# Forgetting attention and a two-layer GELU network on one core: rebuilt fronts of the first two batches, another order in a second GEMM, and earlier loads

## The chip, the cores and the metric

The kernel runs on one core of a Trainium2 chip. The metric is the device time of one execution in microseconds (us); less is better. The kernel before was timed three times: 337.19, 337.76 and 339.93 us, median 337.76. The engines are named as in the profile: PE (TensorE, matmul), PEld (its weight load), DVE (VectorE), ACT (ScalarE), POOL (GpSimd) and SP (SyncE, which here only issues DMAs).

## The reference

```python
# q, k, v: [8, 8, 576, 64], f: [8, 8, 576] in 0.8..1.0
scores = scale * q @ k.T
cum    = cumsum(log(clip(f, 1e-4, 1)))
scores = where(causal, -1e9, scores + cum[:, None] - cum[None, :])
attn   = softmax(scores)                 # per batch and head
x      = (attn @ v) -> [8 * 576, 512]
out    = gelu(x @ w_in) @ w_out          # w_in [512, 2048], w_out [2048, 512]
```

The term of the query in the decay cancels in the softmax. So the kernel multiplies v by a weight for each key, which is proportional to exp(-cum), carries the weight itself as a 65th column of v, and divides by that column's sum at the end.

## The kernel before

**Tiling.** Work goes batch by batch. The eight heads of a batch are four pairs (i = 0 to 3). The 576 keys are five blocks of 128 (the last two overlap by 64 keys). For each pair, `scores` makes four tiles of scores (t = 0 to 3) on PE into the two-buffer PSUM pool "s"; ACT takes the exponential of each tile; the causal mask is laid on afterwards by POOL (`affine_select`, L312), or beforehand by small extra matmuls on PE where `on_pe` holds. `attend` multiplies the exponentials with the weighted v (`vw`), one head at a time, into pool "o"; `normalize` (two DVE instructions) gives x. x is transposed into xT, by PE and a copy in batches 0 and 1, by a DMA on SP in the others. Then the first GEMM (`gemm1`, 16 steps of four matmuls, each with a GELU on ACT) makes the tiles g. The second GEMM (`gemm2_...`) of a batch runs as filler between the score tiles of the next batch: `take(fill, n)` issues its next n steps.

The last 64 rows of each batch are gathered in `tails` and go through both GEMMs at the end of the kernel.

**PSUM.** There are three pools of two buffers: "s", "o" and "m". A new tile in a pool waits until the tile two places before it has been read.

**The order of work.** Every engine works its own instructions in the order in which the code issues them, which is written out by hand. The queues matter as much as the engines:

- SP issues the loads of v (`load_v`, L120, five DMAs for each call, one for each block of keys), the transposes by DMA (`transpose_dma` L236, `x_dma` L370) and the stores of the output (`store`, L506).
- POOL issues the loads of q and k (`load_qk_tokens`, L108), of w_in in four quarters (L172) and of w_out in four quarters (L176). Between these it weighs v (`weigh_v`, L269 and L276) and masks (L312). A tiny copy holds its queue until a transfer has landed (`gate` L568, `behind` L573).
- There is one v_sb. A new batch of v can be loaded only after `weigh_v` has read the old one.

**The front, batch 0 (`first_attention`).** ACT takes the log of f (L187), DVE sums it up (L189), ACT takes the exponential (L588, L191 brings its table), PE transposes the weights (L598). q and k of each pair are transposed by PE (`transposes_first`) and copied by DVE, or by ACT for the first pair (L217 to L222). After `gate`, POOL issues the loads of w_in, v and q, k of batch 1, and the first quarter of w_out.

**Batch 1 (`second_attention`).** Filler is `gemm2_first(0)`: for the row blocks ts = 0 and 1 of batch 0, the steps kt = 0 to 7 of sixteen. This uses the first two quarters of w_out (kt 0 to 3 and 4 to 7). The last two quarters are loaded near its end.

**Batch 2.** Filler is `gemm2_third`: `gemm2_second(0)` (kt 8 to 15 for ts 0 and 1), then PLAN_0 (all of kt for ts 2 and 3 of batch 0), then PLAN_1 (batch 1). A step marked "r" in a plan is two matmuls of 64 rows each into two banks; one marked "n" is one of 128 rows. The two banks are copied and added by DVE into a tile `ot` (pool "outs", four buffers) and stored. Batch 2 gives 48 filler steps before its first `attend`. In the first GEMM of batch 1 the code also issues `weigh_v` for the pairs 0 and 1 of batch 2, then the loads of q and k of batch 3.

Of the kernel before, what the change touches and what calls it, by code (L numbers as in the profile page):

```python
# [12 lines left out]
Alu = mybir.AluOpType  # L13
# [40 lines left out]
def kernel(  # L54
# [100 lines left out]
    e4 = [consts.tile([P, 2, 448], BF16, name=f"e4{i}") for i in range(4)]  # L155
    for t in e4:
        nc.gpsimd.memset(t[:, :, 0:D], 0.0)
    diagonal(ident_fp, Alu.not_equal, 1.0, 0)
    load_qk_tokens(0, 6, 8)
# [20 lines left out]
    ones = consts.tile([BH, S], FP32)  # L180
    lf = f_sb
    cum = consts.tile([BH, S], FP32)
    wk = f_sb
    nc.vector.memset(ones, 1.0)
    nc.vector.memset(wT[0:D, 4, :], 0.0)
    nc.vector.tensor_scalar(f_sb, f_sb, 1e-4, 1.0, Alu.max, Alu.min)
    nc.scalar.activation(lf, f_sb, Act.Ln)  # L187
    nc.vector.memset(v_sb[0:D, :, 4, :], 0.0)
    nc.vector.tensor_tensor_scan(cum, ones, lf, 0.0, Alu.mult, Alu.add)  # L189
    spark = consts.tile([1, 1], FP32)  # L190
    nc.scalar.activation(spark, ones[0:1, 0:1], Act.Exp)  # L191

    def warm_up(n):

        ps = m_psum.tile([P, TC], FP32, tag="m", name="ps_w")
        for _ in range(n):
            nc.tensor.matmul(ps, warm[:, 0:P], warm, start=True, stop=True)
# [4 lines left out]
    def transposes_first(b, i, which, pool, tag):  # L202
# [12 lines left out]
        src = ps.rearrange("d j p -> d p j")  # L215
        if b or i:
# [9 lines left out]
    def transpose_dma(b, h0, h1):  # L226
# [8 lines left out]
        for src, dst in zip(qk_of[b], tq_of[b]):  # L235
            nc.sync.dma_start_transpose(  # L236
                dst[:, h0:h1].rearrange("d h j p -> d (h j) p"),
                src[:, h0:h1].rearrange("p h c -> p (h c)"),
            )
# [24 lines left out]
    def weigh_v(b, i, eng=nc.gpsimd):  # L264
# [3 lines left out]
        w = wT[:, :, bh : bh + 2].rearrange("p n h -> p h n")  # L268
        eng.tensor_tensor(  # L269
            vw(b)[:, hs, :, 0:D],  # L270
            v_sb[:, hs, :, :],
            w.unsqueeze(3).to_broadcast([P, 2, NBLK, D]),
# [7 lines left out]
    def scores(b, i, t):  # L280
        on_pe = b == 0 or (b == 1 and i == 0)
# [42 lines left out]
    def attend(b, i, h, ms):  # L324
        if (b, i, h) not in o_of:
            o_of[b, i, h] = o_psum.tile([P, NBLK, D + 1], FP32, tag="o", name="o")
# [125 lines left out]
    PLAN_0 = [(2, "o", 16 * "r"), (3, "m", 14 * "r" + 2 * "n")]  # L452
# [55 lines left out]
    ot_of = []  # L508

    def gemm2_first(c):  # L510

        pss = [
            m_psum.tile([P, d_model], FP32, tag="m", name="ps2") for _ in range(2)
        ]
        for kq in (0, 4):
            for ts in range(2):
                for kt in range(kq, kq + 4):
                    nc.tensor.matmul(  # L518
                        pss[ts],
# [3 lines left out]
                        stop=(kt == 7),  # L523
                    )
                    if kt == 7:
                        ot_of.append(
                            o_pool.tile([P, d_model], FP32, tag="ot", name="ot")
                        )
                        copy = nc.scalar.copy if ts else nc.vector.tensor_copy
                        copy(ot_of[ts], pss[ts])  # L530
                    yield

    def gemm2_second(c):

        for ts, pool, tag in ((0, o_psum, "o"), (1, m_psum, "m")):
            banks = [
                pool.tile([P, d_model], FP32, tag=tag, name="ps2") for _ in range(2)
            ]
            for kt in range(8, n_ff):
                for r in range(2):  # L540
                    rows = slice(r * D, (r + 1) * D)
                    nc.tensor.matmul(  # L542
                        banks[r],
                        g_of[c][kt][rows, ts * P : (ts + 1) * P],
                        w_out_sb[rows, kt, :],
# [300 lines left out]
```

## Time and profile before

| | us |
|---|---|
| Runs | 337.19, 337.76, 339.93 |
| The profiled execution's own time | 337.49 |
| Span of its profile (first to last instruction) | 335.5 |
| PE busy in the span | 326.8 |
| ACT busy | 209.2 |
| DVE busy | 181.2 |
| POOL busy | 122.4 |

The granted clock of TensorE was 0.997 over the span. The profile is read in this order: the page gives the share of each engine; the chain of waits tells in which stretch something other than PE sets the pace; the timeline of one engine gives single instructions, with the idle time ahead of them and what ended it; the DMA view of a narrow window gives one transfer's time from issue to landing. All times are from the start of the span.

### The profile page before, as it was taken

What the parts mean: (1) busy time and instruction counts of PE and PEld (TensorE: products, weight loads), DVE (VectorE), ACT (ScalarE), POOL (GpSimd) and SP (SyncE); (2) the same over time, 40 slices, a digit from 0 to 9 for tenths busy, and PEclk for the clock granted to TensorE, in tenths of its full rate; (3) what the DMA queues carried; (4) which work ended last, traced back from release to release, by engine and by line L of the source; (5) the groups of instructions that cost most, each with busy time, mean ns of one, the idle gap of its engine ahead of it and who ended that gap; (6) DMA issues with size and microseconds to landing.
All of it is one profiled execution on the core that took longest, in us unless ns stands there. A gap on an engine that the chain in (4) does not pass through costs nothing.

```text
span 335.5 us, 7820 instructions
## 1 busy us (share of the span) xinstructions
PE 326.8 (97%) x3161; PEld 171.2 (51%) x3161; DVE 181.2 (54%) x414; ACT 209.2 (62%) x299; POOL 122.4 (36%) x250
## 2 busy tenths in 40 slices
PE   8799989999999999999999999999999999999995
PEld 3574546445554456445644565446544654444443
DVE  4770456684358945894589547964696550020011
ACT  6977797773734787378827891788378846404600
POOL 8190286038437044723463343624351420000000
PEclk9999999999999999999999999999999999999998
DMA  7999999989999799599949698689800241011013
GB/s 113 188 166 191 206 172 165 193 157 169 206 197 177 119 198 189 102 141 148 224 120 141 136 179 174 87 158 211 140 35 2 83 64 61 0 66 62 0 41 84
DMA packets 104627, 44.16 MB, mean 132 GB/s; under 512 B 83408, under 2 KB 100048, under 8 KB 104592
## 3 DMA queue, kind: packets, MB, share of 16 engines
q1 hardware_dynamic: 87296, 29.52, 46.4%
q0 software_dynamic: 16896, 13.63, 27.6%
q8 instruction: 24, 0.39, 0.5%
q10 hardware_dynamic: 400, 0.52, 0.4%
q14 instruction: 11, 0.09, 0.1%
HBM read 36.85 MB, written 9.44 MB: 138 GB/s over the span
## 4 chain that ended last, share of the span: by engine, by line
PE 83%; DMA 10%; POOL 3%; issue 1%; ACT 1%; DVE 1%; SPq 0%; POOLq 0%; DVEq 0%; ACTq 0%
PE ps L386 33%; PE ps L482 26%; PE ps L422 8%; PE o L331 7%; PE s L300 6%; DMA w_out_sb<-in_moe_w_out_dram 6%; DMA xT<-x 2%; DMA v_sb<-in_v_dram 2%; PE ps L542 1%; PE ps L518 1%; POOL q L108 1%; POOL k L108 1%; ACT e L310 1%; POOL vw L269 0%; SPq L120 0%
## 5 line engine op out<-in xcount | busy, mean ns | idle before, releaser
L406 ACT ACTIVATE g<-ps 128x512 bf16<-128x512 f32 x144 | 82.1, 601 | 83.7 <-PE ps L386 83.7
L310 ACT ACTIVATE e<-s 128x896 bf16<-128x896 f32 (+2 forms) x128 | 100.1, 835 | 20.9 <-PE s L300 18.2
L386 PE MATMUL ps<-xT,w_in_sb 128*128 128x512 bf16 x512 | 112.7, 379 | 0.1
L482 PE MATMUL ps<-w_out_sb,g 64*128 64x512 bf16 (+1 forms) x711 | 108.1, 377 | 0.0
L386 PEld LDWEIGHTS <-w_in_sb 128*128 128x128 bf16 x576 | 55.9, 98 | 67.8 <-issue 2.1
L312 POOL TENSOR_SCALAR_AFFINE_SELECT e<-e 128x256 bf16<-128x256 bf16 (+1 forms) x135 | 49.3, 386 | 86.9 <-ACT e L310 86.6
L482 PEld LDWEIGHTS <-g 64*128 64x128 bf16 (+1 forms) x711 | 39.4, 95 | 34.7 <-issue 4.2
L269 POOL TENSOR_TENSOR vw<-v_sb,wT 128x640 bf16<-128x640 f32 x30 | 38.7, 1290 | 26.0 <-DMA v_sb<-in_v_dram 14.7
L300 PE MATMUL s<-qT,kT 64*128 64x320 bf16 (+4 forms) x384 | 43.8, 276 | 2.2 <-ACT e L310 1.3
L250 DVE COPY kT<-tk 64x288 bf16<-64x288 bf16 x96 | 43.9, 458 | 2.3 <-DMA tk<-k 0.7
L250 DVE COPY qT<-tq 64x288 bf16<-64x288 bf16 x96 | 38.8, 404 | 3.7 <-DMA tq<-q 2.3
L490 DVE COPY ot<-ps 128x512 f32<-128x512 f32 x20 | 13.8, 692 | 47.2 <-PE ps L482 47.2
L331 PEld LDWEIGHTS <-e 128*128 128x128 bf16 x960 | 34.5, 98 | 8.6 <-POOL e L312 2.5
L331 PE MATMUL o<-vw,e 128*128 128x65 bf16 x960 | 37.4, 194 | 0.5 <-DVE vw L269 0.5
L345 DVE TENSOR_TENSOR x<-o,r 128x320 bf16<-128x320 f32 x64 | 31.5, 492 | 3.3 <-DMA xT<-x 1.1
L431 DVE COPY ot<-ps 128x512 f32<-128x512 f32 (+2 forms) x9 | 5.7, 633 | 49.6 <-PE ps L422 49.6
L300 PEld LDWEIGHTS <-kT 64*128 64x128 bf16 x384 | 19.6, 94 | 24.1 <-issue 7.6
L422 PE MATMUL ps<-w_out_sb,g 128*128 128x512 bf16 (+2 forms) x144 | 28.0, 355 | 0.0
L422 PEld LDWEIGHTS <-g 128*128 128x128 bf16 x144 | 13.5, 98 | 14.5
L344 DVE RECIPROCAL r<-o 128x5 f32<-128x5 f32 x64 | 12.1, 189 | 12.2 <-PE o L331 12.1
L502 DVE TENSOR_TENSOR ot<-ot,ps 128x512 f32<-128x512 f32 x22 | 15.1, 685 | 1.1
L386 PE MATMUL ps<-tails,w_in_sb 128*128 128x512 bf16 x64 | 14.3, 378 | 0.0
(69 smaller groups left out, 137.5 us busy)
## 6 DMA issues: line engine op xcount, KB each, us to landing
out_dram<-ot SPq DMA_DIRECT2D x32, 256.0 KB, 2.5
v_sb<-in_v_dram SPq DMA_DIRECT2D x24, 256.0 KB, 4.6
q<-in_q_dram POOLq DMA_DIRECT2D x6, 576.0 KB, 6.3
k<-in_k_dram POOLq DMA_DIRECT2D x6, 576.0 KB, 8.2
v_sb<-in_v_dram SPq DMA_DIRECT2D x22, 128.0 KB, 4.6
w_in_sb<-in_moe_w_in_dram POOLq DMA_DIRECT2D x4, 512.0 KB, 8.2
w_out_sb<-in_moe_w_out_dram POOLq DMA_DIRECT2D x4, 512.0 KB, 8.6
q<-in_q_dram POOLq DMA_DIRECT2D x4, 144.0 KB, 4.5
```

The lines of the kernel that those rows point to most:

```text
L250: nc.vector.tensor_copy(rows[:, odd], src[odd * D : (odd + 1) * D, 2 * i + h].rearrange("d j p -> d p j"),)
L269: eng.tensor_tensor(vw(b)[:, hs, :, 0:D], v_sb[:, hs, :, :], w.unsqueeze(3).to_broadcast([P, 2, NBLK, D]), Alu.mult,)
L300: nc.tensor.matmul(to, *ab, start=half < 0, stop=half == 1 or not masked)
L310: nc.scalar.activation(et[:, :, z:c], st[:, :, z:c], Act.Exp, scale=scale)
L312: nc.gpsimd.affine_select(out=et[:, :, c0 + z : c0 + P], in_=et[:, :, c0 + z : c0 + P], compare_op=Alu.is_ge, fill=0.0, base=z, pattern=[[ ...
L331: nc.tensor.matmul(o[:, m, :], e_of[b, i, t][:, h, c : c + P], vw_of[b][:, 2 * i + h, n, :], start=(n == 0), stop=(n == m),)
L345: nc.vector.tensor_tensor(x_of[b, i][:, :, h, :], o[:, :, 0:D], r.unsqueeze(2).to_broadcast([P, NBLK, D]), Alu.mult,)
L386: nc.tensor.matmul(ps, w_in_sb[:, kt, ffb * P : (ffb + 1) * P], src[:, kt, 0:TC], start=(kt == 0), stop=(kt == n_dm - 1),)
L406: nc.scalar.activation(g_of[c][ffb], ps, Act.Gelu)
L422: nc.tensor.matmul(pss[ts][:, c0:c1], g_of[c][kt][:, ts * P : (ts + 1) * P], w_out_sb[:, kt, c0:c1], start=(kt == 0), stop=(kt == n_ff - 1),)
L482: nc.tensor.matmul(banks[r], g_of[c][kt][rows, ts * P : (ts + 1) * P], w_out_sb[rows, kt, :], start=kt == (steps.index("r") if r else 0), ...
L502: nc.vector.tensor_tensor(ot, ot, bank, Alu.add)
```

## The change

It does the following.

- **Weights of v (batch 0).** The log, the running sum and the exponential are replaced by one running product on DVE, from the last key backwards, that starts at 2^80. ACT loads one table instead of two at the start. The filling of four tiles `e4` and of others with zeros moves from POOL to DVE; the loads of the last q and k of batch 0 move ahead of it on POOL.
- **Order in batch 0.** The transposes of q and k are put one at a time between score tiles; the copy of the last k comes behind the weighing of pair 0, which is done in two parts (four blocks, then the last one); the two heads of a pair are attended one after the other, pair 1 in pool "m".
- **Loads for batch 1.** v of batch 1 is loaded as two heads, then two, then four, instead of four and four. The second quarter of w_out moves from the end of batch 0's GEMM to the end of batch 1's attention, where the other two quarters stand. q of batch 2 keeps its place; k of batch 2 is issued later by POOL, behind the masks of pair 1.
- **Order in batch 1.** The third set of transposes comes behind the tiles of pair 0; the masks of pair 3 are made by PE; both heads of pair 3 are attended before the third transpose of x. The table of GELU is brought by an extra tiny activation.
- **Second GEMM of batch 0.** In batch 1 the filler takes kt 0 to 3 for all four ts (also sixteen steps). In batch 2 `gemm2_second` takes the other 48: kt 4 to 7 for ts 0 and 1, kt 8 to 15 for these, then kt 4 to 15 for ts 2, then for ts 3.
- **v of batch 2, and q, k, v of batch 3.** `load_v(2)` moves from the end of batch 1's attention to a place behind the transposes by DMA of q and k of batch 2, which now go q, q, k, k. All four `weigh_v` of batch 2 stand in the first GEMM of batch 1, the loads of q and k of batch 3 between the second and the third. `load_v(3)` stands at the end of that GEMM instead of behind the first `attend` of batch 2.

```diff
-    for t in e4:
-        nc.gpsimd.memset(t[:, :, 0:D], 0.0)
+    load_qk_tokens(0, 6, 8)
     diagonal(ident_fp, Alu.not_equal, 1.0, 0)
-    load_qk_tokens(0, 6, 8)
...
-    nc.scalar.activation(lf, f_sb, Act.Ln)
-    nc.vector.tensor_tensor_scan(cum, ones, lf, 0.0, Alu.mult, Alu.add)
...
-    def scores(b, i, t):
-        on_pe = b == 0 or (b == 1 and i == 0)
+        on_pe = b == 0 or (b == 1 and i in (0, HP - 1))
...
     def gemm2_third():
         yield from gemm2_second(0)
-        yield from gemm2_rows(0, PLAN_0)
         yield from gemm2_rows(1, PLAN_1)
...
-        nc.scalar.activation(
-            wk, cum, Act.Exp, bias=cum[:, S // 2 : S // 2 + 1], scale=-1.0
-        )
-        warm_up(2)
+        nc.vector.tensor_tensor_scan(
+            decay[:, S - 2 :: -1], f_sb[:, S - 1 : 0 : -1], none[:, 0 : S - 1],
+            2.0**80, Alu.mult, Alu.add,
+        )
+        warm_up(2, 2 * P)
...
-        transposes_first(0, 3, 1, m_psum, "m")
-        weigh_v(0, 0, nc.vector)
+        copy = transposes_first(0, 3, 1, m_psum, "m", late=True)
+        weigh_v(0, 0, nc.vector, 0, NBLK - 1)
+        weigh_v(0, 0, nc.vector, NBLK - 1)
+        copy()
...
-        load_v(1, 0, 4)
+        load_v(1, 0, 2)
...
-        heads = [(i, h) for i in range(3) for h in range(2)]
-        for i, t in ((2, 2), (2, 3), (3, 0), (3, 1), (3, 2), (3, 3)):
-            scores(0, i, t)
-            attend_head(*heads.pop(0))
+        scores(0, 2, 2)
+        for ms in ((0, 1, 2, 3), (4,)):
+            for h in range(2):
+                attend(0, 0, h, ms)
+        for h in range(2):
+            normalize(0, 0, h)
+        scores(0, 2, 3)
+        scores(0, 3, 0)
+        for h in range(2):
+            attend_head(1, h, m_psum, "m")
+        scores(0, 3, 1)
+        scores(0, 3, 2)
+        for h in range(2):
+            attend_head(2, h)
+        scores(0, 3, 3)
...
         tiles(0, 0)
-        transposes(1, o_psum, "o")
-        transposes(2, m_psum, "m")
+        transposes(1, m_psum, "m")
+        transposes(2, o_psum, "o")
+        tiles(0, 2)
         transposes(3, o_psum, "o")
-        tiles(0, 2)
         take(fill, 2)
...
         take(fill, 4)
+        load_qk_tokens(2, which="k")
         weigh_v(1, 2)
...
         tiles(3, 0)
-        transpose_dma(2, 0, 4)
-        transpose_dma(2, 4, 8)
+        for n in range(2):
+            transpose_dma(2, 0, 4, (n,))
+            transpose_dma(2, 4, 8, (n,))
+        load_v(2)
...
         tiles(3, 2)
+        nc.scalar.activation(warm[0:1, 0:1], warm[0:1, 0:1], Act.Gelu)
         behind(qk_of[2][1], H - 1)
+        load_w_out(1)
         load_w_out(2)
         load_w_out(3)
         run(2)
         take(fill, 4)
-        av(3, 0)
+        run(3)
...
-        av(3, 1)
...
-        load_v(2)
...
                 if ffb == 12:
                     behind(qk_of[1][0], H - 1)
+                    load_v(1, 2, 4)
                     load_v(1, 4, 8)
                     weigh_v(1, 0)
-                    load_w_out(1)
                     weigh_v(1, 1)
-                    load_qk_tokens(2)
+                    load_qk_tokens(2, which="q")
...
-                if late == gap - 2 and (b > 1 or at < 2):
+                if late == gap - 2:
                     weigh_v(b + 1, at)
                 if ffb == (9 if b == 1 else 14):
                     load_qk_tokens(b + 2)
+                if b == 1 and ffb == n_ff - 1:
+                    load_v(3)
```

In `attention(2)` the calls `load_v(3)` behind the first `attend`, and `weigh_v(2, 2)` and `weigh_v(2, 3)` behind the tiles of pair 0, are gone. The new heart of `gemm2_second`, in short:

```python
order = [(ts, kt) for two in ((0, 1), (2, 3)) for kq in (0, 8) for ts in two
         for kt in range(kq, kq + 8) if kt >= 4]
order.sort(key=lambda at: (2, 3).index(at[0]) if at[0] in (2, 3) else -1)
# ts 0 and 2 in pool "o", ts 1 and 3 in pool "m"; DVE adds both banks to ot, SP stores it
```

## The prediction

> **What bounds the kernel now.** First the page: engine shares.
>
> ```profile
> PE 326.8 (97%) x3161; PEld 171.2 (51%) x3161; DVE 181.2 (54%) x414; ACT 209.2 (62%) x299; POOL 122.4 (36%) x250
> ```
>
> PE is idle for 335.5 - 326.8 = 8.7 us in all. Second, the busy times by stage (width, then PE, PEld, DVE, ACT, POOL, granted clock, DMA share, GB/s), to see where.
>
> ```profile
> 5.20:16.00 10.80, 8.82 (x188) 6.24 (x188) 7.33 (x13) 10.55 (x16) 4.01 (x13) 1.00 1.09 192
> 39.00:57.00 18.00, 16.62 (x289) 10.40 (x282) 10.78 (x25) 15.70 (x21) 15.02 (x29) 1.00 1.17 176
> 70.20:101.70 31.50, 31.50 (x367) 16.55 (x366) 15.71 (x35) 16.45 (x19) 15.84 (x32) 1.00 0.97 177
> ```
>
> The front of batch 0 has 1.98 us to give and batch 1 some 1.4. Batch 2 has nothing: each wait put there lengthens the run. Third, the timeline of the front: the last two waits of PE and the steps on ACT that go.
>
> ```profile
> 4.04 0.68 ACT L187 ACTIVATE f_sb<-f_sb 64x576 f32<-64x576 f32 x1 [1.95 <-DVE f_sb L186]
> 4.74 1.28 ACT L191 ACT_TABLE_LOAD   x1
> 6.91 0.40 ACT L220 COPY kT<-ps_f 128x288 bf16<-128x288 bf16 x1
> 7.20 0.77 ACT L588 ACTIVATE f_sb<-cum 64x576 f32<-64x576 f32 x1
> 7.88 8.63 ACT L310 ACTIVATE e<-s 128x896 bf16<-128x896 f32 x11
> ...
> 15.05 0.37 PE L300 MATMUL s<-qT,kT 64*128 64x448 bf16 x2 [0.33 <-ACT e L310]
> 16.01 0.63 PE L331 MATMUL o<-vw,e 128*128 128x65 bf16 x15 [0.51 <-DVE vw L269]
> ```
>
> Fourth, batch 2: POOL's and SP's queues and the DVE copy that frees PE's banks.
>
> ```profile
> 72.87 1.28 POOL L269 TENSOR_TENSOR vw<-v_sb,wT 128x640 bf16<-128x640 f32 x1 [14.67 <-DMA v_sb<-in_v_dram]
> 75.62 0.84 POOL L108 DMA_DIRECT2D q<-in_q_dram  x1
> 77.23 1.73 POOL L312 TENSOR_SCALAR_AFFINE_SELECT e<-e 128x256 bf16<-128x256 bf16 x5
> 78.94 1.27 POOL L269 TENSOR_TENSOR vw<-v_sb,wT 128x640 bf16<-128x640 f32 x1
> ```
> ```profile
> 73.67 9.45 SPq L506 DMA_DIRECT2D out_dram<-ot  x4
> 84.18 2.18 SPq L370 DMA_TRANSPOSE xT<-x  x1
> 86.45 4.51 SPq L120 DMA_DIRECT2D v_sb<-in_v_dram  x5
> ```
> ```profile
> 86.58 0.69 DVE L490 COPY ot<-ps 128x512 f32<-128x512 f32 x1 [2.56 <-PE ps L482]
> 87.38 0.69 DVE L502 TENSOR_TENSOR ot<-ot,ps 128x512 f32<-128x512 f32 x1
> ```
>
> POOL waits 14.67 us for v of batch 2. The four stores of batch 0 are out of SP's queue before v of batch 3 enters it. The copy at 86.58 is the first that uses an `ot` tile a second time (four buffers), so it needs the first store landed; the sum behind it ends at 88.07, and PE takes the same two banks again at 88.16. No slack there. Fifth, the DMA queues while both carry data, 32 to 36 us (q0 POOL's, q1 SP's), and SP's alone, 66.2 to 72.
>
> ```profile
> q0 software_dynamic: 776, 0.57, 91.3%
> q1 hardware_dynamic: 772, 0.19, 36.5%
> ```
> ```profile
> q1 hardware_dynamic: 5140, 1.29, 130.6%
> ```
>
> Beside POOL's queue SP's moves 0.19 MB in 4 us (48 GB/s), alone 1.29 in 5.8 (222).
>
> **The change part by part.** The sum is made against the profiled execution's 337.49 (span 335.5 and 1.99 around it); the median of the runs, 337.76, is 0.27 above.
>
> *Front of batch 0.* The log (0.68), a table (1.28) and an exponential (0.77) leave ACT. Most of it was cover time: the first tile needs the second half of kT, which ACT copies at 6.91 when DVE's half is done, unchanged. Its scores are done at 7.70, so the first exponential starts at some 7.72 instead of 7.88: 0.16. The running product is one DVE scan, as before (1.35), now behind the kT copy: 6.9 to 8.25, when DVE has no other work until 8.31. The zero fills on DVE (eight of 0.1 to 0.5) lie in its wait for f until 3.56. Weighing pair 0 no longer stands behind the last kT copy (14.46 to 15.22): DVE's four blocks 14.1 to 14.8, the last when it lands (14.75) by 15.0; PE then goes on after its tile at 15.27 instead of 16.01: 0.74. From there PE's work is the same 8.2 us to 24.24, but the last tile's exponential now ends some 0.1 later than the third pair leaves PE. Gain 0.64; bounds 0 (last block of v 0.7 later, since q and k of pair 3 enter POOL's queue 0.95 earlier) and 1.95 (all gaps).
>
> *Batch 1.* v for heads 2 to 7 is moved behind q, so w_out's first quarter lands earlier (42.66 before) and PE's 0.44 us wait for it goes; what is late next is the third set of transposes, which now stands ahead of that place and waits for the copies of the second, with the same end. The extra masks (four small matmuls for a diagonal) put 0.12 behind PE's last tile; attending both heads first gives 0.12 back (wait of the last transpose for x). The GELU table (1.28) was hidden under PE's first matmuls already. On POOL the issue of k (0.78) comes between masks and weighing: last mask of pair 2 at 52.4 where 52.05 was, PE would want it at 52.2. So +0.2; bounds -1.2 (ACT's four gaps) and +1.0 (first rival below). Copies of `ot` on DVE: two more of 0.69, DVE has 7.2 us free here.
>
> *w_out.* Three quarters instead of two issue at some 53.4; two landed 6.8 and 10.3 us after their issue, 4.25 apart. The third lands by 69, needed at 72.5 (twelve steps of 0.216 into batch 2). Nothing. The filler of batch 2 is 48 steps both times: nothing.
>
> *v of batch 2 and SP's queue: the term that decides.* v(2) enters SP's queue earlier, but the bytes ahead of it are the same: the second quarter of w_out is moved into its path. The DMAs are at 90% or more all the way from 30 to 72 us but for some 1.9 us at 54 to 57, and the new order makes a hole of its own, while POOL waits for v's heads 2 and 3 before it issues q(2). It landed at 72.71. I take 72.3 (the exponentials ahead of k's issue are 0.6 earlier); ends 70.8 (no hole) and 75 (three quarters at 4.25 after 53.4, then the 7.1 us that v took after w_out before). POOL then weighs two pairs, issues q and k, weighs two more (before: 72.87 to 77.23, and 2.65 for two): v_sb is free at 79.5, and only then does SP issue `load_v(3)`. In the changed program its five loads stand ahead of the four stores of batch 0, which want to leave at 73.67. From first issue to last landing these five took 7.75 us undisturbed (86.45 to 94.20) and 10.1 in batch 3 (119.35 to 129.46), where a store issued right behind landed 0.27 after them. Here k of batch 3 shares the DMAs (it landed at 85.71) for some 3 us, at 48 instead of 222 GB/s: 7.75 + 3 x 0.78 = 10.05. The first store lands at 79.55 + 10.05 + 0.27 = 89.9, and the copy due at 86.58 starts then: +3.3 on PE. Queued behind it on DVE: the sum, then the normalizing of pair 1; who waits is PE, for both banks, and everything after it. As the copy now hangs on DMAs, the 0.4 gained ahead is lost in the same wait. Ends: no stall (v at 70.8 and 7.75: 86.1), and +5.7 (v at 75).
>
> [...] In this trace the store behind v in batch 3 landed after it. [...]
>
> Sum: 337.49 + 3.3 = 340.8.
>
> **The rivals.** (1) *The stores are in time*: v(2) lands below 69, or overtaking. Decides when the first store lands before 86. For it: v enters SP's queue earlier. Against it: the same bytes, DMAs full. Then the front's gain stays: 337.49 - 0.64 + 0.2 = 337.05, down to 335.5 if batch 1 gains too. This is the other side. (2) *POOL late in batch 1*: v of heads 2 and 3 is issued only after q's landing (38.34 before); if it lands later than 42.5, weighing (1.5), q(2) and the five masks (1.7) push the attend of pair 1, 1 us for each. For it: such loads took 4.5 us then. Against: the POOL queue is then empty. 338.0 if the stores are in time. (3) *Masks of batch 2 late*: all four weighings now stand ahead; masks end 9.1 us after v(2) lands, PE wants them at 81.2; above 72.1 it is the wait that shows first. Alone: 337.5 at 72.7. (4) *Wide DMA delay*: v(2) at 75 or w_out late: 343.2.
>
> **How the numbers follow.** Forecast (stores late by 1 to 5 us) 0.70; rival 1 0.19; rivals 2 and 3 without it 0.06; rival 4 0.05. Within 1% is about what a measurement can tell from no change: against 337.76 this is 334.4 to 341.1, so the forecast stands near its edge. Of its 0.70, 0.35 is above 341.1 (v(2) landing above 72.6); with 0.05 of rival 4 and 0.01, slower is 0.41. Faster by over 1% needs batch 1 to give over 2 us: 0.03. Within 1%: 0.56. The range goes from 336.5 (rival 1 with half of what batch 1 can give) to 343.0 (v(2) near 75); the forecast's own is 338.5 to 343.
>
> **What would show it.** Right: the DVE copy of `ot` in the first row block of PLAN_1 idle until a DMA of `out_dram`, PE idle some 3 us behind it near 88 us, SP's five loads of v ahead of four stores near 80; PE's first attend near 15.3; no wait of PE for w_out at 42.7. Wrong: v(2) landed and weighed before 70, the four stores out by 76, batch 2 without idle time on PE; or the loss in batch 1 at the attend of pair 1 or 2.

## The result and the profile after

The changed kernel takes 347.65 us (median of 6 runs, 346.40 to 348.56), the kernel before 338.06 (6 runs): ratio 1.028 with a 95% interval of 1.024 to 1.031. The forecast was 340.8 with a range to 343.0. The sign and the place were right, the size was not. Here and below a ratio is to the kernel before, run beside it on the same chip; it is taken by rounds and leaves disturbed executions out (e5's profiled execution is one of these), so that it can differ from the ratio of the medians.

The profiled execution of the changed kernel took 348.56 us, that of the kernel before 337.49: 11.07 more. First the engine shares on the page of the changed kernel, and the row of its clock in 40 slices of 8.7 us.

```profile
PE 326.9 (94%) x3139; PEld 173.5 (50%) x3179; DVE 181.9 (52%) x422; ACT 206.7 (60%) x297; POOL 119.8 (35%) x241
...
PEclk9999999999889999999999999999999999999999
```

PE's busy time on the page is that of before (326.8), but that can't be read as "all of the loss is idle time": the page has 3139 matmuls beside 3179 weight loads, so records are missing, and part of the busy time now runs at half clock (slices 11 and 12, 87 to 104 us). The busy times by stage (same columns as before) say where the loss lies.

```profile
5.20:16.00 10.80, 9.17 (x214) 6.67 (x214) 7.75 (x13) 9.36 (x13) 3.28 (x8) 1.00 1.04 180
39.00:57.00 18.00, 15.84 (x307) 10.97 (x311) 12.03 (x28) 16.45 (x23) 12.05 (x24) 1.00 0.98 153
70.82:102.00 31.18, 25.37 (x249) 12.96 (x252) 14.85 (x36) 12.39 (x15) 12.48 (x25) 0.89 0.88 169
```

Batch 2, where PE had no idle time before, now has 5.8 us of it, at a mean clock of 0.89. By the first score matmuls of each batch in the timeline, batch 2 begins at 70.82 (before 70.10) and lasts 55.61 us (45.37). So 0.72 comes ahead of it, 10.24 in it, 0.39 behind it, and -0.28 outside the span: 11.07.

The chain behind this, in the timelines of the changed kernel: POOL, SP, DVE, then PE. (v(2) is v of batch 2, and so on.)

```profile
77.10 1.28 POOL L271 TENSOR_TENSOR vw<-v_sb,wT 128x640 bf16<-128x640 f32 x1 [18.17 <-PE s L302]
79.84 0.84 POOL L108 DMA_DIRECT2D q<-in_q_dram  x1
82.83 1.28 POOL L271 TENSOR_TENSOR vw<-v_sb,wT 128x640 bf16<-128x640 f32 x1
84.21 2.68 POOL L314 TENSOR_SCALAR_AFFINE_SELECT e<-e 128x256 bf16<-128x256 bf16 x8
```
```profile
64.11 28.65 SPq L120 DMA_DIRECT2D v_sb<-in_v_dram  x10
92.81 2.12 SPq L507 DMA_DIRECT2D out_dram<-ot  x4
```
```profile
96.11 0.69 DVE L491 COPY ot<-ps 128x512 f32<-128x512 f32 x1 [8.25 <-DMA out_dram<-ot]
```
```profile
77.42 0.37 PE L561 MATMUL ps<-w_out_sb,g 64*128 64x512 bf16 x1 [0.56 <-DVE ot L570]
78.14 1.88 PE L561 MATMUL ps<-w_out_sb,g 64*128 64x512 bf16 x15 [0.35 <-DVE ot L503]
...
84.66 0.23 PE L333 MATMUL o<-vw,e 128*128 128x65 bf16 x2 [0.72 <-POOL e L314]
85.62 1.32 PE L333 MATMUL o<-vw,e 128*128 128x65 bf16 x28 [0.73 <-POOL e L314]
...
96.85 0.37 PE L483 MATMUL ps<-w_out_sb,g 64*128 64x512 bf16 x1 [2.62 <-DVE ot L491]
97.64 1.86 PE L483 MATMUL ps<-w_out_sb,g 64*128 64x512 bf16 x7 [0.42 <-DVE ot L503]
```

v(2) landed at 76.76 (before 72.71); POOL starts weighing 0.34 us behind it (its row names PE's scores as the last event before, but in e7, e8 and e13 the row names the load, with the same 0.34), has weighed the last pair by 84.1, and SP issues the five loads of v(3) from 84.14, all ten loads of v standing in one row of SP's queue. The four stores, whose first sum is done at 78.1, leave at 92.81; the first lands at 96.02, and the copy that wants its `ot` tile waits for it as forecast (before: at 86.58, without). PE waits 3.04 us there. But it waits in three places: 0.91 for DVE's sums before that, and 1.45 for the masks, which stand on POOL behind four weighings. These are 5.40 us. The clock costs some 3.2 more: the granted clock is 0.50 in 87.0 to 90.4 and in 97.3 to 100.7 ("half clock" below), and PE is busy for 3.4 and 3.1 us of these.

```profile
83.60:87.00 3.40, 1.86 (x33) 1.22 (x34) 1.67 (x4) 0.00 (x0) 3.29 (x10) 1.00 1.32 202
87.00:90.40 3.40, 3.40 (x20) 1.27 (x18) 0.82 (x3) 1.62 (x2) 0.64 (x2) 0.50 1.25 237
```

The remaining 1.6 us of the 10.24 go in the main with the same waits, by an estimate from these rows. A matmul of L561 alone lasts 0.37 us, fifteen in a row 1.88 (78.14), so in a row the next one starts after 0.11. The work ahead of a wait counts as busy to its end, 0.16 to 0.26 us beyond the point at which PE would have gone on; over six waits that is some 1.2 us. e1 and e2, without a half clock, have such a rest too: batch 2 is 3.31 us longer with 2.17 of idle waits (four) in e1, 3.04 with 2.52 (two) in e2.

### The profile page after: what moved, and what is told of

Its sections match the earlier page's. It is cut to its first block, busy times and chain, and to the rows that moved or that the text cites. A ratio compares the mean times of both kernels' runs of the same rounds, so it can differ in the third digit from the quotient of the medians.

```text
span 346.8 us, 7818 instructions
## 1 busy us (share of the span) xinstructions
PE 326.9 (94%) x3139; PEld 173.5 (50%) x3179; DVE 181.9 (52%) x422; ACT 206.7 (60%) x297; POOL 119.8 (35%) x241
## 4 chain that ended last, share of the span: by engine, by line
PE 68%; SPq 9%; DMA 9%; POOL 5%; issue 5%; DVE 2%; ACT 0%; POOLq 0%; DVEq 0%; ACTq 0%
PE ps L388 27%; PE ps L483 22%; PE ps L424 8%; PE o L333 6%; SPq L120 5%; PE s L302 5%; DMA v_sb<-in_v_dram 4%; SPq L238 4%; POOL vw L271 2%; DMA q<-in_q_dram 2%; DMA xT<-x 1%; POOL q L108 1%; POOL k L108 1%; DMA out_dram<-ot 1%; DVE x L347 0%
## 5 line engine op out<-in xcount | busy, mean ns | idle before, releaser
L483 PE MATMUL ps<-w_out_sb,g 64*128 64x512 bf16 (+1 forms) x631 | 100.4, 387 | 4.5 <-DVE ot L491 2.6
L314 POOL TENSOR_SCALAR_AFFINE_SELECT e<-e 128x256 bf16<-128x256 bf16 (+1 forms) x130 | 47.4, 384 | 96.5 <-ACT e L312 96.4
L483 PEld LDWEIGHTS <-g 64*128 64x128 bf16 (+1 forms) x649 | 37.9, 97 | 36.3 <-issue 9.7
L302 PE MATMUL s<-qT,kT 64*128 64x320 bf16 (+4 forms) x384 | 45.2, 278 | 3.6 <-ACT e L312 2.5
L252 DVE COPY kT<-tk 64x288 bf16<-64x288 bf16 x96 | 41.8, 436 | 8.9 <-DMA tk<-k 7.3
L252 DVE COPY qT<-tq 64x288 bf16<-64x288 bf16 x96 | 40.1, 417 | 1.4
L491 DVE COPY ot<-ps 128x512 f32<-128x512 f32 x18 | 12.5, 692 | 51.0 <-PE ps L483 42.7
L302 PEld LDWEIGHTS <-kT 64*128 64x128 bf16 x384 | 20.6, 95 | 24.5 <-issue 8.5
L503 DVE TENSOR_TENSOR ot<-ot,ps 128x512 f32<-128x512 f32 x22 | 15.1, 685 | 1.1
```

Of the source, the lines that this page charges most:

```text
L252: nc.vector.tensor_copy(rows[:, odd], src[odd * D : (odd + 1) * D, 2 * i + h].rearrange("d j p -> d p j"),)
L302: nc.tensor.matmul(to, *ab, start=half < 0, stop=half == 1 or not masked)
L314: nc.gpsimd.affine_select(out=et[:, :, c0 + z : c0 + P], in_=et[:, :, c0 + z : c0 + P], compare_op=Alu.is_ge, fill=0.0, base=z, pattern=[[ ...
L483: nc.tensor.matmul(banks[r], g_of[c][kt][rows, ts * P : (ts + 1) * P], w_out_sb[rows, kt, :], start=kt == (steps.index("r") if r else 0), ...
```

## The experiments

Theory at the start: v(3) stands ahead of the stores on SP, and the weighings ahead of the masks on POOL; taken away, nearly all of the loss goes. Rivals: w_out's move, the order of the transposes by DMA, the new order of the work itself. Start and length of batch 2 are from the one profiled execution. v(2) and w_out: landing of their last piece. The column "us" is the median of all runs of the kernel.

| kernel | us | ratio (95%) | batch 2 starts | lasts | w_out | v(2) |
|---|---|---|---|---|---|---|
| before | 338.06 | 1 | 70.10 | 45.37 | 65.60 | 72.71 |
| changed | 347.65 | 1.028 (1.024-1.031) | 70.82 | 55.61 | 69.29 | 76.76 |
| e1 | 340.73 | 1.0065 (1.004-1.009) | 69.31 | 48.68 | 67.64 | 75.05 |
| e2 | 339.94 | 1.0051 (1.002-1.009) | 69.64 | 48.41 | 67.28 | 73.74 |
| e3 | 347.18 | 1.0269 (1.024-1.030) | 74.46 | 50.32 | 68.62 | 74.97 |
| e4 | 344.66 | 1.0190 (1.015-1.023) | 73.44 | 51.65 | 69.11 | 74.74 |
| e5 | 341.39 | 1.0060 (1.002-1.011) | 70.57 | 50.73 | 71.99 | 79.62 |
| e6 | 338.96 | 1.0015 (0.999-1.004) | 70.73 | 45.37 | 67.31 | 74.63 |
| e7 | 346.95 | 1.025 (1.019-1.031) | 69.69 | 56.86 | 68.98 | 76.01 |
| e8 | 344.36 | 1.0124 (1.005-1.020) | 73.28 | 51.65 | 73.29 | 79.72 |
| e9 | 339.56 | 1.0005 (0.997-1.004) | 70.44 | 45.51 | 67.07 | 74.33 |
| e10 | 339.40 | 1.0012 (0.998-1.005) | 72.31 | 45.36 | 69.38 | 75.85 |
| e11 | 346.50 | 1.0212 (1.016-1.027) | 70.81 | 55.15 | 66.09 | 72.69 |
| e12 | 339.98 | 1.0047 (1.002-1.008) | 70.04 | 47.73 | 68.10 | 76.04 |
| e13 | 347.80 | 1.0272 (1.021-1.033) | 70.83 | 56.37 | 70.65 | 78.11 |
| e14 | 343.97 | 1.0168 (1.014-1.020) | 72.16 | 50.65 | 66.22 | 72.82 |

**e1, v(3) back behind the first attention of batch 2.**

```diff
-                if b == 1 and ffb == n_ff - 1:
-                    load_v(3)
...
                     av(i - 1)
+                    if b == 2 and i == 1:
+                        load_v(3)
```

> The changed kernel with load_v(3) back behind the first attend of batch 2, all else as changed. Theory (the stores of batch 0 wait in SP's queue behind v of batch 3): the DVE copy of the first row block of PLAN_1 no longer idles 8.25 us, PE's 3.0 us of waits at 94 to 98 us go, and so does the 3.4 us of half clock that followed them (worth 1.7): 347.65 - 4.7 = about 343. The masks' wait near 85 us and the half clock from 87.0 stay. Rival A (the wait for the store is only cover, another wait of batch 2 takes its place): 346 to 347.5. Rival B (all of the loss in batch 2 hangs on this one load): 338.5.

6.9 of the 9.6 us go, more than expected: in the profiled execution no half clock is left. The copy of `ot` no longer waits for a store. What remains in batch 2 are 0.71 for DVE's sums and 1.46 for the masks.

**e2, the weighing of pairs 2 and 3 back in batch 2 as well**, on top of e1.

```diff
-                if late == gap - 2:
+                if late == gap - 2 and (b > 1 or at < 2):
...
+                if b == 2 and (i, t) == (0, 3):
+                    weigh_v(b, 2)
+                    weigh_v(b, 3)
```

> As e1, and the weighing of pairs 2 and 3 of batch 2 back behind the tiles of pair 0 in batch 2 (as in the kernel before). Theory (four weighings ahead of the masks make PE wait at its first attend, and that wait draws the first half clock): a further 1.5 us of waits and 1.7 of half clock go: about 339.8, no half clock in batch 2. Rival (masks stay late because v of batch 2 lands at 76.8 anyhow): masks of pair 0 end 76.8 + 2.8 + 1.6 + 1.7 = 82.9 where PE wants them at 83.5, so little is left; if it is wrong, 341.5 to 343.

The time is as expected, the waits are not: that for the masks goes, but PE now waits 2.17 and 0.35 us for DVE's sums, so hardly anything is gained over e1. In this execution v(2) landed 1.3 us sooner than in e1, and POOL's weighing (from 74.08) fell beside DVE's last "untangling" copies, which sort the transposed tq and tk into qT and kT: four of them took 3.42 us, those before them 1.34.

```profile
73.64 3.42 DVE L252 COPY kT<-tk 64x288 bf16<-64x288 bf16 x4
```

e11 and e14 follow this up.

**e4, that part alone put into the kernel before**: four weighings in batch 1's GEMM and v(3) at its end.

```diff
-                if late == gap - 2 and (b > 1 or at < 2):
+                if late == gap - 2:
...
+                if b == 1 and ffb == n_ff - 1:
+                    load_v(3)
```

> The kernel before with one part of the change alone: all four weighings of batch 2 in the first GEMM of batch 1 and load_v(3) at its end. v of batch 2 lands at 72.7 as before. Theory: the masks end at 81.8 where PE wants them at 81.6 (0.2 to 0.7 us), the first store lands some 19 us after v of batch 2, at 91 to 92.5, so the copy due at 86.6 waits 5 us and PE about 4, and one stretch of half clock follows (1.7): 338.06 + 5.7 = about 343.5. Rival (without w_out in its path the part is free): 338.

As expected: +6.3 us, the first store at 93.7, a wait of 2.84 us for the copy of `ot`, 0.21 behind it, and a half clock of 6.8 us.

```profile
94.50 0.58 PE L482 MATMUL ps<-w_out_sb,g 64*128 64x512 bf16 x1 [2.84 <-DVE ot L490]
95.29 1.86 PE L482 MATMUL ps<-w_out_sb,g 64*128 64x512 bf16 x7 [0.21 <-DVE ot L502]
```

Batch 2 is 6.28 us longer: 3.05 of waits and, since PE was busy for some 5.7 of the 6.8 us, some 2.8 for the clock. And v(2) was not late here: it landed 1.3 us after the start of batch 2 (before: 2.6). So the order on SP and POOL costs this much even with v(2) in time. (That batch 2 starts at 73.44 has another cause: in this execution the last q and k of batch 0 landed late, 14.03 and 15.75 instead of 12.22 and 13.38, with 6.8 us of half clock from 15.1.)

**e7, the four stores on ScalarE's queue**, all else as in the changed kernel.

```diff
     def store(c, ts, ot):
-        nc.sync.dma_start(out[c * S + ts * P : c * S + (ts + 1) * P, :], ot)
+        eng = nc.scalar if c == 0 else nc.sync
+        eng.dma_start(out[c * S + ts * P : c * S + (ts + 1) * P, :], ot)
```

> The changed kernel, with the four stores of batch 0's result issued on ScalarE's queue instead of SyncE's; all loads stay where the change put them. Theory (the stores come late because SyncE issues in order and stands at the five loads of v(3), 84.1 to 92.8): the first store lands before 86 to 88, the copy ot is not late by more than 1 us, no half clock, 341 to 342.5, what is left being the late masks and the late kT. Rival (the stores are late because the DMA engines' work comes late or is shared, or a copy ot is late by itself): first store not landed before 93, 346 to 348.

The first store landed at 79.75, and still nothing was gained. The timeline of ACT shows the fourth.

```profile
82.12 0.34 ACTq L508 DMA_DIRECT2D out_dram<-ot  x1
82.56 0.81 ACT L312 ACTIVATE e<-s 128x768 bf16<-128x768 f32 x1 [1.60 <-DVE ot L503]
92.02 0.34 ACTq L508 DMA_DIRECT2D out_dram<-ot  x1
92.46 2.56 ACT L312 ACTIVATE e<-s 128x896 bf16<-128x896 f32 x3 [9.09 <-DMA v_sb<-in_v_dram]
```

The program hands eight semaphores round among the DMAs of SP and ACT (108 and 112 to 118; in the trace of the changed kernel too the first load of v(3) and the fourth store behind it both have 114). The fourth store had that of the first load of v(3) and waited for it to land (91.94). ACT's exponentials stood behind it for 9.09 us, and PE for 5.06, with 6.8 us of half clock. The order of a queue had come back as the order of a semaphore.

**e8, three stores on ScalarE's queue, the fourth on SyncE's.** The diff is that of e7 with `c == 0 and ts < 3`.

> The changed kernel with the first three of the four stores of batch 0's result on ScalarE's queue and the fourth left on SyncE's, behind the loads of v(3). In e7 the first three were issued at 77.7, 79.0 and 82.1, but the fourth waited on ScalarE until 92.0: it carries the DMA semaphore (114) that the first load of v(3) had taken, and that load landed at 91.94. So ScalarE's exponentials stood behind it, and TensorE waited 5.06 us. Theory (the store behind v(3) is the largest term, and e7 only moved the wait to another engine): the first store lands before 82, the copy ot is not late, no half clock, 340 to 342.5; what is left are the late masks and the late kT (e1 had 2.2 us of such waits). Rival (with v(3) loaded this early something else stands in the stores' place, whatever their queue): 345 to 347.5.

Between the two by the median; by its ratio (1.0124) at the upper end of the theory. The copy waits for no store any more and batch 2 is 4.0 us shorter than in the changed kernel; then the masks come into the open, as the prediction's third rival had it, with 6.8 us of half clock behind them. This execution's v(0) and v(2) were late besides (v(2) 79.72).

```profile
87.62 0.29 PE L333 MATMUL o<-vw,e 128*128 128x65 bf16 x2 [2.64 <-POOL e L314]
88.59 1.91 PE L333 MATMUL o<-vw,e 128*128 128x65 bf16 x28 [0.67 <-POOL e L314]
```

**e3, w_out's second quarter back in batch 0's GEMM**, else the changed kernel.

```diff
                     weigh_v(1, 0)
+                    load_w_out(1)
                     weigh_v(1, 1)
...
-        load_w_out(1)
         load_w_out(2)
```

> The changed kernel with the load of the second quarter of w_out back at the end of batch 0's first GEMM; load_v(3) and the four weighings stay where the change put them. Theory (the common root is that this quarter, moved into the path of the transposes and of v of batch 2, makes v land at 76.8 instead of 72.7): v lands 3 to 4 us sooner, the masks' wait goes, the store lands near 92 and PE waits some 1 to 3 us there: 340 to 342. Rival (the order of SP's queue alone decides, however early v lands): 343 to 345. Rival (the quarter of w_out delays q of batch 2 just as much): 347.

Missed. v of batch 1's heads 2 and 3, which the change moved to the same place, now landed at 45.8 instead of 42.6, and PE waited 2.56 us for masks behind their weighing: the prediction's second rival, with 6.8 us of half clock. So in the changed kernel w_out's move makes room for v(1). v(2) landed at 74.97, 1.8 us sooner than in the changed kernel, and still PE waited 2.74 us for the store, with 3.4 of half clock. That the time met the second rival's 347 was chance: its cause was another.

**e6, the new front and orders, every load as before**: v(1) in two halves, w_out and k(2) at their old places, transposes q, k, q, k, v(2) and v(3) late.

```diff
-        load_v(1, 0, 2)
+        load_v(1, 0, 4)
...
-                    load_v(1, 2, 4)
                     load_v(1, 4, 8)
                     weigh_v(1, 0)
+                    load_w_out(1)
                     weigh_v(1, 1)
-                    load_qk_tokens(2, which="q")
+                    load_qk_tokens(2)
...
-        for n in range(2):
-            transpose_dma(2, 0, 4, (n,))
-            transpose_dma(2, 4, 8, (n,))
-        load_v(2)
+        transpose_dma(2, 0, 4)
+        transpose_dma(2, 4, 8)
...
```

> The changed front, the changed order of TensorE's work in batch 1 and the changed order of the second GEMM of batch 0, with every load, transpose and weighing of batches 1 to 3 at its place in the kernel before (v of batch 1 in halves, w_out's second quarter in batch 0's GEMM, q and k of batch 2 together, v of batch 2 and 3 late). Theory (the front brings what it was priced at, and only the moved loads cost): 337.3 to 337.9, that is 0.4 to 0.9 below the kernel before. Rival 1 (the front's gain is lost again in the wait of batch 2's first copy, since the loads there are not earlier): 338.1, the same. Rival 2 (the new order of the work itself costs): 339 or more.

The same as before: all of the loss is in the moved loads, transposes and weighings, but the front's gain isn't there either. The number is rival 1's, the place is not: batch 2 lasts 45.37 us as before, but starts 0.63 later. In this execution PE waited 0.79 us for x of batch 0 (at 23.27), 0.67 for k(1) and 0.18 for w_out.

**e9, the front alone**: from batch 0's first GEMM on everything as before.

```diff
-    nc.scalar.activation(lf, f_sb, Act.Ln)
...
-        nc.scalar.activation(
-            wk, cum, Act.Exp, bias=cum[:, S // 2 : S // 2 + 1], scale=-1.0
+        nc.vector.tensor_tensor_scan(
+            decay[:, S - 2 :: -1],
...
+        for ms in ((0, 1, 2, 3), (4,)):
+            for h in range(2):
+                attend(0, 0, h, ms)
```

> Only the front of batch 0 changed (the weights by a running product on VectorE in place of logarithm and exponential on ScalarE, the memsets moved, the new order of scores and attention); everything from the first GEMM of batch 0 on as in the kernel before. Theory (the front is worth what the prediction gave it, 0.64): 337.3 to 337.8. Rival (what it gains in the front is lost behind it, in the wait for w_out at 42.7 and behind the late loads): 338.0 to 338.5. If e9 shows the gain and e6 did not, the new order of batch 1 costs it.

No measurable difference. The timeline of PE shows the gain and its loss.

```profile
15.40 1.12 PE L333 MATMUL o<-vw,e 128*128 128x65 bf16 x30
...
23.44 12.35 PE L388 MATMUL ps<-xT,w_in_sb 128*128 128x512 bf16 x56
...
36.67 0.45 PE L207 MATMUL ps_f<-key_of,k 96*64 96x96 bf16 x12 [0.51 <-DMA k<-in_k_dram]
...
40.79 0.45 PE L207 MATMUL ps_f<-key_of,k 96*64 96x96 bf16 x12 [1.16 <-DMA k<-in_k_dram]
...
43.35 0.60 PE L520 MATMUL ps<-w_out_sb,g 128*128 128x512 bf16 x2 [1.01 <-DMA w_out_sb<-in_moe_w_out_dram]
```

The long row of batch 0's GEMM starts at 23.44 (before 24.24), and then PE meets loads that don't come any sooner: 2.68 us of waits for k(1) and w_out, where it had 0.44. Batch 2 starts at 70.44, later than before.

**e10, e6 with w_out's second quarter late**, and **e11, e6 with the transposes in the order q, q, k, k**. e11 also writes `load_v(2)` earlier, but SP's queue has nothing else between: in the order of instructions only the transposes differ.

```diff
-                    load_w_out(1)
...
+        load_w_out(1)
         load_w_out(2)
```
```diff
-        transpose_dma(2, 0, 4)
-        transpose_dma(2, 4, 8)
+        for n in range(2):
+            transpose_dma(2, 0, 4, (n,))
+            transpose_dma(2, 4, 8, (n,))
+        load_v(2)
```

> e6 with one step more: the load of w_out's second quarter moved from batch 0's GEMM to the two others in batch 1, as the change has it; nothing else. Theory (three quarters of w_out beside the four transposes by DMA make the late kT that e2 and e5 had): the second half of tk lands 2 to 4 us later than in e6 (69.1), VectorE's copy ot makes TensorE wait 1 to 2.5 us near 78, 339.5 to 341 against 338.96 of e6. Rival (it is v of batch 2, loaded earlier beside them): no wait near 78, within 0.5 of e6.

> e6 with v(2) loaded ahead of the third tile of pair 3's scores and the transposes by DMA in the order q, q, k, k, as the change has them; w_out, v(1), k(2) and everything else as in e6. Theory (w_out's third load is what makes the kT late, not v(2)): within 0.5 of e6's 338.96. Rival (the earlier v(2) or the order of the transposes makes it late): tk lands over 2 us later, a wait of 1 to 2.5 us near 78, 339.5 to 341.

My theory of w_out fell: e10 is within 0.5 us of e6 and has no wait near 78 (in its profiled execution PE waited 1.23 us for w_out at 43.9 instead, with 3.4 of half clock). In e11 the order of the transposes costs 7.5 us by itself (6.7 by the ratios). DVE, POOL and PE in e11:

```profile
66.30 1.35 DVE L252 COPY kT<-tk 64x288 bf16<-64x288 bf16 x4 [6.43 <-DMA tk<-k]
...
71.73 1.34 DVE L252 COPY kT<-tk 64x288 bf16<-64x288 bf16 x4
73.09 3.70 DVE L252 COPY qT<-tq 64x288 bf16<-64x288 bf16 x4
76.80 5.59 DVE L252 COPY kT<-tk 64x288 bf16<-64x288 bf16 x4
82.42 0.69 DVE L570 TENSOR_TENSOR ot<-ot,ps 128x512 f32<-128x512 f32 x1
```
```profile
72.86 1.34 POOL L271 TENSOR_TENSOR vw<-v_sb,wT 128x640 bf16<-128x640 f32 x1 [13.86 <-DMA v_sb<-in_v_dram]
...
77.42 1.82 POOL L314 TENSOR_SCALAR_AFFINE_SELECT e<-e 128x256 bf16<-128x256 bf16 x5
79.22 1.27 POOL L271 TENSOR_TENSOR vw<-v_sb,wT 128x640 bf16<-128x640 f32 x1
```
```profile
83.16 4.29 PE L561 MATMUL ps<-w_out_sb,g 64*128 64x512 bf16 x16 [6.32 <-DVE ot L570]
```

With both q transposes first, the first k lands at 66.27, in the kernels with q, k, q, k at 56.7 to 64.2, and DVE stands for 6.43 us. The untangling copies then fall into POOL's weighing and masks, and four copies take 3.70 and 5.59 us instead of 1.34 (one copy 3.41 instead of 0.33). The sums come late, PE waits 6.32 us, and the clock is halved for 10.2. e1 and e2 have the same order and lose far less; v(2) lands later in them (72.69 here, 73.74 in e2, 75.05 in e1): six copies are lengthened in e11, two in e2, none in e1.

**e5, e2 with the transposes in the order q, k, q, k.**

```diff
-        for n in range(2):
-            transpose_dma(2, 0, 4, (n,))
-            transpose_dma(2, 4, 8, (n,))
+        transpose_dma(2, 0, 4)
+        transpose_dma(2, 4, 8)
         load_v(2)
```

> e2 with the four transposes by DMA of batch 2 back in the order q, k, q, k, and nothing else. In e2 the only wait of TensorE over 0.2 us left in batch 2 was for VectorE's copy ot (2.17 and 0.35 us near 78), with VectorE still untangling the late kT at that time (the halves of tk had landed at 65.4 and 68.2; in the kernel before at 59.75 and 67.30). Theory (the order of the transposes keeps VectorE's untangling late): the first half of tk lands near 60-62, the 2.2 + 0.35 us go, 337.6 to 338.4. Rival (the transposes are late because the five loads of v(2) run beside them, whatever their order): 339.5 to 340, with the same wait near 78.

Inconclusive. Four of ten runs lie at 338.1 to 339.1, the others at 341.3 and above, where the kernel before spreads from 336.8 to 341.0 beside it. In the profiled one, at 343.43, k(2) landed at 57.11 (54.23 in the changed kernel), and everything behind it late, so it can't decide between theory and rival.

**e13, the same in the changed kernel itself.** The diff is that of e5.

> The changed kernel with nothing undone but the order of the four transposes by DMA, back to q, k, q, k. e11 showed that this order alone costs 7 us when all else is as before: VectorE waits 6.4 us for the first kT, so its untangling copies fall into the time of GpSimd's weighing, and copies of 0.33 us then take 1.3 to 3.4. In the changed kernel v(2) lands so late (76.76) that the weighing starts only after the untangling (76.64). Theory (in the changed kernel the order is worth no more than the waits of 0.56 and 0.35 us, the late v(2) and what follows it are the main cost): 345.5 to 347.5. Rival (the order is the root here too): 339 to 342.

As the theory had it: nothing gained. In the changed kernel v(2) is so late that its weighing (77.10) starts when the untangling has just ended (76.64), so the late v(2) hides this collision. Each of the two moves costs 6 to 7.5 us alone (e4, e11), and the whole change 9.6: they don't add up.

**e14, e11 with the eight last untangling copies on ScalarE.**

```diff
     def untangle(b, i):
+        copy = nc.scalar.copy if b == 2 and i == HP - 1 else nc.vector.tensor_copy
...
-                    nc.vector.tensor_copy(
+                    copy(
```

> e11 (346.5; the same as e6 on SyncE's queue but for the order q, q, k, k of the transposes by DMA), with the eight copies that untangle q and k of pair 3 of batch 2 on ScalarE instead of VectorE; nothing else. In e11 these eight ran from 73.09 to 82.39 instead of 2.7 us: those that ran beside GpSimd's weighing took 1.29, 1.44, 1.03 and 3.41 us instead of 0.33. Theory (VectorE's copies stand while GpSimd works on its tiles, and the ot sums behind them make TensorE wait 6.3 us and halve its clock): on ScalarE the eight copies keep one duration, whether GpSimd works or not, VectorE's first ot sum is no later than 77, the wait of 6.3 us and the half clock go, 338.7 to 340.5. Rival (the copies are late for another reason, as their data or the DMA): they are lengthened on ScalarE as well, and it stays over 344.

ACT, POOL and PE of e14:

```profile
71.89 2.12 ACT L253 COPY qT<-tq 64x288 bf16<-64x288 bf16 x4
74.04 2.12 ACT L253 COPY kT<-tk 64x288 bf16<-64x288 bf16 x4
```
```profile
72.99 1.37 POOL L272 TENSOR_TENSOR vw<-v_sb,wT 128x640 bf16<-128x640 f32 x1 [12.73 <-DMA v_sb<-in_v_dram]
74.47 1.27 POOL L272 TENSOR_TENSOR vw<-v_sb,wT 128x640 bf16<-128x640 f32 x1
```
```profile
76.83 1.09 PE L562 MATMUL ps<-w_out_sb,g 64*128 64x512 bf16 x7 [3.23 <-ACT g L409]
```

The theory holds for the copies: eight of 0.51 us each, six of them beside POOL's multiplies. The time was missed by 3.5 us, since these 4.3 us on ACT stood ahead of the last GELU, and PE waited 3.23 us for it, with 3.4 us of half clock behind.

**e12, the best of both as the runs pointed to it**: e6 with v(1) in the change's pieces, and w_out's second quarter between q(2) and k(2).

```diff
...
                     weigh_v(1, 0)
-                    load_w_out(1)
                     weigh_v(1, 1)
-                    load_qk_tokens(2)
+                    load_qk_tokens(2, which="q")
+                    load_w_out(1)
+                    load_qk_tokens(2, which="k")
```

> e6 (front and orders of the change, loads of batches 2 and 3 as before) with v of batch 1 in the change's three pieces and w_out's second quarter between q and k of batch 2. Theory (e6 and e9 lost the front's 0.5 to 0.8 us in waits for k(1) and w_out of 0.7 to 2.2 us at the start of batch 1, which e1 and e2 did not have, since less of v(1) lies ahead of k(1); and batch 2 needs the transposes in the order q, k, q, k and w_out's second quarter out of their way): batch 1 starts at 37.7 to 38.0, batch 2 at 69.3 to 69.7, batch 2 takes 45.4, 336.9 to 337.7 against about 338.2 of before. Rival (the DMA engines have no slack left for it; k(2) or tk comes later by the piece of v(1) moved, and the kT with it): 338.2 to 339.5.

The rival won, and the median lies above even its range. The waits for k(1) and w_out went, but v(2) landed at 76.04, POOL issued q(3) and k(3) 1.6 us later than in e6, and SP's transposes of x with them: PE waits 1.23 us for `xT` at the start of batch 2's GEMM. No version that was run beats the kernel before.

## Why the prediction was wrong

Right by its own steps:

- The front: first attention at 15.27 forecast, 15.19 measured (15.3 to 15.7 in e1 to e3), and 0.64 of gain forecast, 0.5 to 0.8 at the start of batch 1 in e1 to e3. In the changed kernel's own profiled execution v(0) landed late and PE waited 1.66 at 20.35. That the gain is lost again was forecast too, though in batch 2; where no late store takes it, k(1) and w_out do (e9).
- Batch 1: +0.2 forecast, 0.0 measured (31.64 us; 31.62 before); no wait for w_out at 42.7.
- w_out's third quarter "lands by 69": 69.29.
- The mechanism: v(3) ahead of the stores, the copy of `ot` waiting for a store, PE behind it. POOL's chain from v(2) to the first load of v(3): 7.2 forecast, 7.38 measured. The store landed after all the loads (0.69 us). Rival 1 also counted on a store that overtakes the loads. The traces of both kernels show none: of SP's transfers (136 before, 141 in the changed kernel) and ACT's (5 and 5) each landed after those issued before it on its queue.

The step that failed is "It landed at 72.71. I take 72.3", argued from "the bytes ahead of it are the same". It landed at 76.76, and in the five profiled executions with the same loads ahead of it (changed, e1, e2, e7, e8) at 73.74 to 79.72, never by 72.3. The argument counted bytes; the rows show what lay last. In all 16 profiled executions v(2) landed 5.6 to 7.9 us after w_out's last quarter, whatever the order (table). The trace of before had this row (65.60 and 72.71). k(2), behind which w_out's late quarters are issued, landed at 54.23 in both kernels, since its own issue had been moved from 44.09 to 47.99; so three quarters started where two had (54.52), and the last landed at 69.29. w_out's cost of "Nothing" was true for w_out alone. Why the distance is so steady is not shown; an estimate from the prediction's own rows fits it: at 48 GB/s beside POOL's queue most of v(2) (1.18 MB) is still to come when w_out has landed, and at 222 GB/s all of it takes 5.3 us. The bound of 75 was meant in just this way, but its sum doesn't give 75: with its own "lands by 69" it is 69 + 7.1 = 76.1. The prediction took the other, earlier end.

The other terms of the sum that were too small: the loads of v(3) took 11.19 us instead of 10.05, the store 0.69 instead of 0.27 more. k of batch 3 shared the DMAs with these loads for 5.4 us (84.14 to its landing at 89.54), where the sum had "some 3 us"; by its own numbers (79.55, and 85.71 less 0.4) it was over 5. Together the copy came at 96.11 instead of 89.9.

By this chain alone PE gets past the store 26.03 us after the start of batch 2 (96.85) instead of 18.06 (88.16): 7.97 of the 10.24. The chain from v(2) over POOL and SP to the store does not pass through PE. So the waits for the sums and masks and the first half clock, which lie ahead of 96.85, are inside these 7.97: without them PE would have stood longer at the store. That PE's wait there (3.04) is close to the forecast 3.3 is luck; the copy came 6.2 us later than forecast, and PE came late to it as well.

What the sum had no term for is the half clock. e4 shows what it is worth where v(2) is in time: there the first store lands 20.2 us after the start of batch 2, where the forecast had it (89.9, batch 2 from some 69.7), PE's waits are 3.05, about as forecast, and batch 2 is 6.28 longer and not 3.3, since some 2.8 for the clock follow. So even with v(2) in time the time would have been some 343.8 (337.49 + 6.28, an estimate; e4 took 344.66), above the range, which ended at 343 because v(2) was bounded at 75 and the clock had no price. In the changed kernel itself, of the 10.24 us 3.3 are the forecast's, some 4.7 (the rest of the 7.97) the late v(2) and the slower loads and store, and 2.3 lie behind the store's copy, the second half clock above all. Rival 3, the late masks, came true beside the forecast and not in its place; in the changed kernel the store covered it (1.45 us), in e1 (1.46) and e8 (3.3) it stood in the open.

What is open: why v(2) follows w_out at so steady a distance, and why its landing spreads by 6 us over executions with the same program ahead.

## What to carry to other kernels

When a load is moved, look up in the trace which transfer it used to land behind, and price the move by that one's new landing, not by a sum of bytes; then follow every queue that waits for the load, since each was in time only by the old landing. A wait that goes may have covered another (store, masks, untangling here): price rivals together, and read by stage which comes next. Where TensorE was never idle, add the clock as a risk to the price of waits that together leave it idle for some 1.5 us or more of 3.4: in the changed kernel half clock followed two of three such stretches (those of 1.54 and 2.67 us idle, not that of 1.58) and in e11 one of 2.06, in e1 it did not follow one of 1.55. At the granted 0.50 it costs 1.7 us for each 3.4 that PE works at it.

## What the runs showed of the hardware that was not expected

- **DVE's copies took longer beside POOL's multiplies.** In the kernel before, 153 untangling copies that ran beside no POOL instruction took at most 0.33 us (median 0.325). Of the 39 beside one, 24 took longer, up to 1.45, all but one of these beside a multiply of the weighing; beside its small cast alone they kept 0.33. In e11 one took 3.41, over within 0.2 us of the end of POOL's last multiply. On ACT they kept 0.51 (e14). What holds DVE's copies up there is not shown.
- **Half a clock after short waits.** In the 3.40 us ahead of the half clock at 87.0 PE was busy for 1.86, with waits of 0.72 and 0.73 us. In e1 the same two waits (0.73 and 0.73) were followed by no half clock, with PE busy for 1.85 us from 82.0 to 85.4. In the trace of the changed kernel the clock records begin at 5.11 (full), 87.03 (half), 90.45, 97.27 (half) and 100.69 us, which is 24, 1, 2 and 1 times 3.413 us from one to the next; in that of before at 6.11 (full) and, 96 times 3.413 us later, at the kernel's end (333.79, half). With the changed kernel's trace cut at these distances, and its end left out, three stretches at full clock have PE busy for under 2.0 us: 1.83 (18.8 to 22.2), 1.87 (83.6 to 87.0) and 0.74 (93.9 to 97.3). The last two were followed by half clock, the first was not; the trace of before has no such stretch. Why some are followed and others not is not shown.
- **Two busy queues moved nearly as many packets, but not as many bytes.** In the prediction's row for 32 to 36 us POOL's queue and SP's moved 776 and 772 packets, but 0.57 and 0.19 MB; in the changed kernel, from 58.5 to 62 us, they moved 515 and 512 packets, 0.51 and 0.13 MB. SP's packets, some 250 bytes each by these numbers, came to 48 GB/s in the first row, against 222 alone.
- **Landings spread widely over executions.** In five kernels with the same program ahead of them (changed, e1, e2, e7, e8) w_out's last quarter landed up to 6.0 us apart (67.28 in e2, 73.29 in e8) and v(2) 6.0 (73.74 in e2, 79.72 in e8). So a landing read from one profiled execution is uncertain by some microseconds.
